# The order of one attention step in a fused attention, token-mixing and MLP kernel: products with V two pairs back, low part of x one step later, first weight blocks decoded later

## The chip, the cores and the metric

The kernel runs on one core of a Trainium2 chip. A core has a matrix engine (PE, with its weight loads shown as PEld), a vector engine (DVE), a scalar engine (ACT), GpSimd (POOL) and a queue engine (SP) that here issues the DMAs. Each engine works through its own instructions strictly in the order in which they were written, and waits at an instruction until the data that it names is there. The metric is the device time of one execution in microseconds (us); less is better. Three runs of the kernel before gave 899.58, 904.35 and 904.69 us, the median is 904.35.

## The reference

Causal attention over 4 batches and 12 heads of 64, then a mixing of tokens through rank 32, then an MLP, with two residual sums:

```python
scores = where(mask, -1e9, q @ k.T / 8)         # 4 x 12 heads, 448 x 448, causal
attn   = exp(scores - max) / (sum + 1e-9)
x      = (attn @ v), heads side by side          # 4 x 448 x 768
u      = x + (x.T @ U @ V).T                     # U 448 x 32, V 32 x 448
out    = u + relu(u @ w_ch1) @ w_ch2             # 768 -> 3072 -> 768
```

The weights arrive as 64-bit floats, so the kernel decodes each block to 32-bit words itself.

## The kernel before, in words

Heads are worked in pairs: a pair is two heads, there are 6 pairs to a batch and 24 in all. The program goes through steps n = -2, -1, 0, ...; a table called `plan` in `attention()` (L918 to L950) lists what one step does, and each entry has a lag: an entry with lag 1 works in step n on pair n - 1. The order of the entries in the table is the order of the instructions on every engine. A step before the change consists of:

- `scores` (L204), lag 0: 8 matmuls of q and k of the pair, causal blocks of 112 rows, into six PSUM banks (tiles `s`).
- `scores_max` (L228) on DVE, one for each block: it adds the mask, writes the block to SBUF (tile `p`) and takes the row maximum; `scores_exp` (L245) on ACT then takes the exponential in place and its row sum. The head of even number is called head 0, the other head 1.
- `sums_inverse` (L252) on DVE and `normalise` (L258) on POOL divide `p` by the row sums.
- `transposes` (L265), lag 1: ten PE transposes for each head into three banks (tiles `t`), which `transposed` (L275) copies to SBUF (tile `pt`), two copies of each head on ACT and one on DVE.
- `values` (L280), lag 1: the products of `pt` with V (tile `pv`); `values_out` (L310) copies them on ACT into x (tiles `xa` for batches 0 and 1, `xb` for 2 and 3).
- `x_natural` (L316), lag 2: four transposes of x (tile `xt`); `natural_high` (ACT) and `natural_low` (DVE) split it into a high part `xn_h` and a low part `xn_l`.
- `low_rank` (L331), for every second pair: 8 matmuls with U (tile `y`), with a high part on ACT and a low part on DVE. `mix` and `mix_sum` (L352 to L360): products with V of the low rank (tile `hm`), two of them in each of three steps of six, and their sum into x on DVE. `split_u` and `split_u_low` on POOL prepare x as the operand of the MLP.

The first 17 steps (n below `START`) run by themselves: this is the front of the kernel, where attention alone keeps the engines busy. What is left of the list of entries is then spread evenly over the MLP of batches 0 and 1 (`mlp()`), which yields after each half of an accumulation; that is the middle. A last part works the MLP of batches 2 and 3 in another form (`strassen()`); the change does not touch it.

Beside the plan, a list named `early` puts pieces of weight preparation into the front: `VU_AT` says at which steps the small matrices U and V are loaded, decoded and split, `W_AT` at which steps blocks 0 and 1 of the weights are decoded (`decode_bits`, L144: two passes on ACT, three on DVE; `decode_sum` on POOL) and split (`split`, one cast on ACT and one subtraction on DVE). These pieces are written directly behind the first entry of their step, so they stand ahead of that step's `scores_max` on DVE and ahead of its exponentials on ACT. In the middle each weight block is decoded in the same way, while the block before is used.

PSUM has eight banks (`bank()`); a new tile takes a bank whose tile before has been read for the last time.

Of the kernel before, what the change touches and what calls it, by code (L numbers as in the profile page):

```python
# [47 lines left out]

MIX, MIXN = 3, 2
START = 17
VU_AT = (0, 2, 2, 3)
UFREE = 60
UGAP = 3
LOADS = (13, 11, 7)
# [3 lines left out]
HE = {"d": "V", "o": "V", "13": "V", "24": "V"}  # L60
UE = {"d": "P", "o": "P", "13": "P", "24": "V"}
WL_AT = (1, 2)
W_AT = (4, 4, 5, 5, 6)


@with_exitstack
def attention_mix_mlp(ctx: ExitStack, tc: tile.TileContext, qk, v, w1, w2, vu, out):
# [48 lines left out]
    def f(ap):  # L116
        return ap.bitcast(F32)
# [6 lines left out]
    def constants():  # L124
        make_identity(nc, ident)
        nc.gpsimd.memset(mask, 0.0)
        nc.gpsimd.affine_select(
            out=mask[:, S - CP :],
            in_=mask[:, S - CP :],
            pattern=[[-1, CP]],  # L130
            compare_op=ALU.is_ge,
            fill=-8.0e9,
            base=0,
            channel_multiplier=1,
        )
# [68 lines left out]
    def scores(b, c):  # L204


        t = st.pop(("qk", b, c))
        room = {}
        for half, i in SCORES:
            h = 2 * c + half  # L210
            n = (i + 1) * CP
            key = half, BANK_OF[half][i]
            if key not in room:
                room[key] = [bank("s")[:CP], 0]
            o, at = room[key]
            room[key][1] = at + n
            o = st["o", b, h, i] = o[:, at : at + n]
            r = slice(half * D, (half + 1) * D)
            nc.tensor.matmul(  # L219
                o,  # L220
                t[r, 0, i * CP : (i + 1) * CP],
                t[r, 1, :n],
                start=True,
                stop=True,
                skip_group_check=True,
            )

    def scores_max(b, h, i):  # L228
        if ("p", b, h) not in st:
            st["p", b, h] = p_p.tile([CP, 1120], F32, tag="p", name="p")  # L230
            st["m", b, h] = p_sm.tile([CP, NT], F32, tag="m", name="m")
            st["l", b, h] = p_sm.tile([CP, NT], F32, tag="l", name="l")
        n = (i + 1) * CP
        nc.vector.tensor_tensor_reduce(  # L234
            out=st["p", b, h][:, POFF[i] : POFF[i] + n],
            in0=st.pop(("o", b, h, i)),
            in1=mask[:, S - n :],
            scale=-(D**-0.5),
            scalar=3.0e38,
            op0=ALU.add,  # L240
            op1=ALU.min,
            accum_out=st["m", b, h][:, i : i + 1],
        )
# [624 lines left out]
    def attention():  # L868


        def of_pair(f, lag):
            def steps(n):
                if 0 <= n - lag < len(pairs):
                    yield f, pairs[n - lag]

            return steps

        def of_tiles(f, half, lag, tiles):
            def steps(n):
                if 0 <= n - lag < len(pairs):  # L880
                    b, c = pairs[n - lag]
                    for i in tiles:
                        yield f, (b, 2 * c + half, i)

            return steps

        def of_head(f, half, lag):
            def steps(n):
                if 0 <= n - lag < len(pairs):
                    b, c = pairs[n - lag]  # L890
                    yield f, (b, 2 * c + half)

            return steps

        def of_two(f, lag):
            def steps(n):
                if 0 <= n - lag < len(pairs) and (n - lag) % 2:
                    b, c = pairs[n - lag]
                    yield f, (b, c // 2)

            return steps

        def mixes(f, part):
            def steps(n):
                for b in range(B):
                    for c in range(NC):
                        if n == b * NPAIR + NPAIR - 1 + MIX + c // MIXN and c % MIXN == part:
                            yield f, (b, c)

            return steps  # L910

        def only(f, *a):
            b, _ = a
            if b < 2:
                f(*a)

        first, second = (0, 2, 3, 1), (1, 3, 2, 0)
        plan = [  # L918
            of_pair(load_qk, -2),
            of_pair(scores, 0),  # L920
            of_tiles(scores_max, 0, 0, first),
            of_tiles(scores_exp, 0, 0, first),
            of_pair(x_natural, 2),
            of_pair(natural_high, 2),
            of_tiles(scores_max, 1, 0, second),
            of_head(sums_inverse, 0, 0),
            of_pair(natural_low, 2),
        ]
        for half in range(2):
            for i in range(3):  # L930
                plan.append(of_tiles(transposes, half, 1, (i,)))
                plan.append(of_tiles(transposed, half, 1, (i,)))
        plan += [
            of_tiles(normalise, 0, 0, first),
            of_tiles(scores_exp, 1, 0, second),
            of_two(low_rank, 2),
            of_two(low_rank_high, 2),
            of_two(low_rank_low, 2),
        ]
        for part in range(MIXN):  # L940
            plan += [mixes(mix, part), mixes(mix_sum, part)]
        plan += [
            of_pair(values, 1),
            of_head(sums_inverse, 1, 0),
            of_tiles(normalise, 1, 0, second),
            of_pair(values_out, 1),
            of_pair(load_v, 0),
        ]
        for part in range(MIXN):
            plan += [mixes(lambda *a: only(split_u, *a), part), mixes(lambda *a: only(split_u_low, *a), part)]  # L950
        def scores_and_max(b, c):
            scores(b, c)
            for half, i in SCORES:
                scores_max(b, 2 * c + half, i)

        def nothing(*_):
            pass

        among = {scores: scores_and_max, scores_max: nothing}
        todo = []  # L960
        for n in range(-2, len(pairs) + 8):
            for steps in plan:
                todo += [(n, f if n < START else among.get(f, f), a) for f, a in steps(n)]
        return todo

    with tc.manual_schedule():
        constants()
        early = [(n, low_rank_weights, (i,)) for i, n in enumerate(VU_AT)]
        early += [(n, load_w, (i,)) for i, n in enumerate(WL_AT)]
        for n, steps in zip(  # L970
            W_AT,
            (
# [7 lines left out]
            early += [(n, step, a) for step, a in steps]  # L980
        early.sort(key=lambda e: e[0])
        todo = attention()
        while todo[0][0] < START:
            n, step, a = todo.pop(0)
# [77 lines left out]
```

## Time and profile before

| what | value |
|---|---|
| median of three runs | 904.35 us |
| profiled execution, its own time | 902.12 us |
| its span, first to last instruction | 900.3 us |
| PE busy | 868.5 us (96%) |
| PEld, DVE, ACT, POOL busy | 84%, 76%, 53%, 35% |
| chain that ended last | PE 80%, DVE 12%, ACT 4% |
| front, 0 to 155.2 us: PE busy | 136.23 us |
| middle, 155.2 to 420 us: PE busy | 264.80 of 264.80 us |
| 420 to 460 us: PE busy | 36.31 of 40 us |
| rest, 460 to 900 us: PE busy | 431.15 of 440 us |

Busy time is the time in which an engine executes; for PE it includes matmuls that overlap, so a busy PE need not be at its peak. The chain is followed back from the last instruction, at each step to what released it. The table shows that PE stands still for 19 us in the front, for 3.7 us shortly after 420 us, and for 9 us in the last part.

### The profile page before, as it was taken

Reading aid. Unit: us, or ns where it says so; the run is one execution under the profiler, and the core shown is the slowest. Engines: PE = TensorE matmul, PEld = TensorE weight load, DVE = VectorE, ACT = ScalarE, POOL = GpSimd, SP = SyncE. Lnnn points to the kernel's source line nnn. Section 1 sums busy time; section 2 is a strip of 40 time slices with the busy share of each in tenths; the row PEclk is TensorE's granted clock in tenths of the full one; section 3 lists DMA queues with packets and bytes.
Section 4 is the critical chain, followed back from the end, with each engine's and each line's share of the span. In section 5 each row is a group of like instructions: output and inputs, shape, how many; then the busy total and the mean of one; then the engine's idle time right before and its main releaser. Section 6 shows DMA issues by size and latency. Waiting matters only on the chain.

```text
span 900.3 us, 13531 instructions
## 1 busy us (share of the span) xinstructions
PE 868.5 (96%) x4728; PEld 756.7 (84%) x4728; DVE 679.9 (76%) x1368; ACT 473.0 (53%) x1002; POOL 315.3 (35%) x342
## 2 busy tenths in 40 slices
PE   6789999999999999999899999999999999999998
PEld 4567777988889898888799999998999898898887
DVE  4766767675766776666478788789988989988896
ACT  5878887544536454355244545365463635445530
POOL 4545847423222222232114424323324323333230
PEclk9989999999999999999899999999999999999999
DMA  6135232244344433434334445612211321212103
GB/s 229 52 115 157 82 94 63 106 136 162 133 151 144 168 126 129 145 116 146 128 106 158 158 158 190 226 42 75 66 54 36 94 59 42 76 48 71 36 1 123
DMA packets 47061, 98.99 MB, mean 110 GB/s; under 512 B 4240, under 2 KB 25744, under 8 KB 46992
## 3 DMA queue, kind: packets, MB, share of 16 engines
q1 hardware_dynamic: 46992, 98.12, 33.3%
q8 instruction: 37, 0.61, 0.3%
q14 instruction: 32, 0.26, 0.1%
HBM read 73.73 MB, written 24.38 MB: 109 GB/s over the span
## 4 chain that ended last, share of the span: by engine, by line
PE 80%; DVE 12%; ACT 4%; issue 2%; DMA 1%; SPq 0%; POOL 0%; DVEq 0%; ACTq 0%
PE hf L424 20%; PE of L449 20%; PE sa L656 14%; PE se L656 7%; PE pv L288 6%; PE s L219 4%; PE sb L656 3%; DVE p L234 3%; PE t L272 3%; DVE h L470 2%; PE y L337 1%; DVE tmp L470 1%; DVE sw L470 1%; DVE xb L470 1%; DVE wsp L470 1%
## 5 line engine op out<-in xcount | busy, mean ns | idle before, releaser
L449 PE MATMUL of<-g,wsp 128*128 128x448 f32 x864 | 184.7, 369 | 0.0
L470 POOL TENSOR_TENSOR wsp<-wld,wsp 128x512 fp32r<-128x512 f32 (+1 forms) x60 | 105.2, 1762 | 215.4 <-ACT wsp L593 132.0
L449 PEld LDWEIGHTS of<-g,wsp 128*128 128x128 f32 x864 | 160.1, 188 | 14.3
L157 POOL TENSOR_TENSOR wa<-wld 128x768 int32<-128x768 int32 (+1 forms) x49 | 73.1, 1492 | 243.6 <-issue 89.7
L261 POOL TENSOR_SCALAR p<-p,r 112x112 f32<-112x112 f32 (+1 forms) x192 | 97.4, 526 | 108.9 <-DVE r L256 69.6
L248 ACT ACTIVATE p<-p,m 112x112 f32<-112x112 f32 (+1 forms) x192 | 99.8, 528 | 25.0 <-DVE m L234 25.0
L656 PE MATMUL sa<-h,wsp 128*128 128x448 f32 x432 | 98.6, 367 | 1.9 <-DVE xb L470 1.9
L424 PE MATMUL hf<-wsp 128*128 128x448 f32 x432 | 95.4, 370 | 0.0
L424 PE MATMUL hf<-u,wsp 128*128 128x448 f32 x432 | 95.4, 370 | 0.0
L656 PE MATMUL sa<-uch,wsp 128*128 128x448 f32 x288 | 89.5, 371 | 3.5 <-ACT r L677 3.5
L452 DVE TENSOR_TENSOR xa<-of,xa 128x448 f32<-128x448 f32 x96 | 59.1, 621 | 40.8 <-PE of L449 40.6
L656 PEld LDWEIGHTS sa<-h,wsp 128*128 128x128 f32 x432 | 80.6, 188 | 10.6 <-DVE xb L470 4.0
L424 PEld LDWEIGHTS hf<-u,wsp 128*128 128x128 f32 x432 | 80.7, 189 | 6.9 <-issue 0.3
L424 PEld LDWEIGHTS hf<-wsp 128*128 128x128 f32 x432 | 79.5, 188 | 7.3
L234 DVE CUSTOM_DVE_ANT_0 p<-s,mask 112x112 f32<-112x112 f32 (+2 forms) x192 | 73.2, 445 | 16.3 <-PE s L219 16.1
L175 ACT CAST wsp<-wa 128x768 fp32r<-128x768 f32 x48 | 40.1, 835 | 79.3 <-POOL wa L157 69.4
L176 DVE TENSOR_TENSOR wsp<-wa,wsp 128x768 fp32r<-128x768 f32 x48 | 50.7, 1057 | 24.7 <-ACT wsp L175 24.7
L432 ACT ACTIVATE g<-hf 128x448 fp32r<-128x448 f32 x48 | 26.1, 544 | 80.0 <-PE hf L424 80.0
L433 DVE SCALAR_TENSOR_TENSOR g<-hf,g 128x448 fp32r<-128x448 f32 x48 | 29.9, 623 | 50.4 <-ACT g L432 50.2
L288 PE MATMUL pv<-pt,v 112*64 112x336 f32 (+3 forms) x384 | 59.1, 434 | 8.5 <-DVE pt L166 6.3
L272 PE MATMUL t<-ident,p 112*112 112x112 f32 x480 | 58.0, 262 | 7.4 <-DVE m L234 4.1
L656 PEld LDWEIGHTS sa<-uch,wsp 128*128 128x128 f32 x288 | 54.0, 188 | 11.7 <-ACT r L677 6.7
(93 smaller groups left out, 1597.7 us busy)
## 6 DMA issues: line engine op xcount, KB each, us to landing
wld<-in_w_dram SPq DMA_DIRECT2D x48, 768.0 KB, 4.6
kept<-wa SPq DMA_DIRECT2D x48, 384.0 KB, 2.6
qk<-in_qk_dram SPq DMA_DIRECT2D x24, 448.0 KB, 3.5
wld<-kept SPq DMA_DIRECT2D x24, 384.0 KB, 3.2
wld<-kept SPq DMA_DIRECT2D x72, 128.0 KB, 2.4
v<-in_v_dram SPq DMA_DIRECT2D x24, 224.0 KB, 3.7
out_dram<-xa SPq DMA_DIRECT2D x12, 224.0 KB, 2.2
out_dram<-xb SPq DMA_DIRECT2D x12, 224.0 KB, 1.9
```

Source lines behind the costliest of these rows:

```text
L157: nc.gpsimd.tensor_tensor(a.bitcast(I32), t[:, :n, 1].bitcast(I32), t[:, :n, 0].bitcast(I32), op=ALU.add)
L176: nc.vector.tensor_tensor(lo, src, f(hi), op=ALU.subtract)
L234: nc.vector.tensor_tensor_reduce(out=st["p", b, h][:, POFF[i] : POFF[i] + n], in0=st.pop(("o", b, h, i)), in1=mask[:, S - n :], scale=-(D* ...
L248: nc.scalar.activation(pi, pi, AF.Exp, bias=m[:, i : i + 1], scale=-1.0, accum_out=l[:, i : i + 1])
L261: nc.gpsimd.tensor_scalar(pi, pi, r[:, i : i + 1], 1.0, op0=ALU.mult, op1=ALU.mult)
L272: nc.tensor.transpose(o[:, n : n + CP], src, ident[:CP, :CP])
L288: nc.tensor.matmul(o[j * D : (j + 1) * D, kt * CP : S], v[:, kt, j, :], pt[:, n0 : n0 + S - kt * CP], start=j not in begun, stop=not left[ ...
L424: nc.tensor.matmul(o, a[:, cs], m, start=(kc + n == 0), stop=(kc + n == NC + 1))
L449: nc.tensor.matmul(o, a[:, cs], m, start=(fc + n == 0), stop=(fc + n == FC + 1))
L452: nc.vector.tensor_tensor(x, o, x, op=ALU.add)
L470: (nc.vector if e == "V" else nc.gpsimd).tensor_tensor(o, a, b, op=op)
L656: nc.tensor.matmul(st[bank, q], a, b, start=(n in FIRST and ms[0] == 0 and k == 0), stop=(n in LAST and end and k == len(steps) - 1), skip ...
```

## The change

In a step, the products with V now belong to the pair two steps back (lag 2 in place of 1) and stand right behind the scores; the transposes of head 0 follow, then the transpose of x, then the transposes of head 1. The last two exponentials of head 1 move behind the copies of head 0. The low part of x is taken one step later (lag 3), and so are `low_rank` (lag 3) and `mix` (`MIX` 4). V is loaded one step later. `START` is 18: one step more runs in the front. U and V of the low rank are finished one step later, and the five pieces of weight decoding move from steps 4, 4, 5, 5 and 6 to steps 7 to 11.

```diff
--- before.py
+++ after.py
@@ -48,9 +48,9 @@
 
 
 
-MIX, MIXN = 3, 2
-START = 17
-VU_AT = (0, 2, 2, 3)
+MIX, MIXN = 4, 2
+START = 18
+VU_AT = (0, 2, 3, 4)
 UFREE = 60
 UGAP = 3
 LOADS = (13, 11, 7)
@@ -60,7 +60,7 @@
 HE = {"d": "V", "o": "V", "13": "V", "24": "V"}
 UE = {"d": "P", "o": "P", "13": "P", "24": "V"}
 WL_AT = (1, 2)
-W_AT = (4, 4, 5, 5, 6)
+W_AT = (7, 8, 9, 10, 11)
 
 
 @with_exitstack
@@ -914,40 +914,43 @@
             if b < 2:
                 f(*a)
 
+        def third(half):
+            plan = []
+            for i in range(3):
+                plan.append(of_tiles(transposes, half, 1, (i,)))
+                plan.append(of_tiles(transposed, half, 1, (i,)))
+            return plan
+
         first, second = (0, 2, 3, 1), (1, 3, 2, 0)
         plan = [
             of_pair(load_qk, -2),
             of_pair(scores, 0),
             of_tiles(scores_max, 0, 0, first),
             of_tiles(scores_exp, 0, 0, first),
+            of_pair(natural_low, 3),
+            of_tiles(scores_max, 1, 0, second),
+            of_tiles(scores_exp, 1, 0, second[:2]),
+            of_pair(values, 2),
+            of_pair(values_out, 2),
+            of_head(sums_inverse, 0, 0),
+            of_tiles(normalise, 0, 0, first),
+            *third(0),
+            of_tiles(scores_exp, 1, 0, second[2:]),
             of_pair(x_natural, 2),
+            of_head(sums_inverse, 1, 0),
+            of_tiles(normalise, 1, 0, second),
+            *third(1),
+            of_two(low_rank, 3),
+            of_two(low_rank_high, 3),
+            of_two(low_rank_low, 3),
             of_pair(natural_high, 2),
-            of_tiles(scores_max, 1, 0, second),
-            of_head(sums_inverse, 0, 0),
-            of_pair(natural_low, 2),
-        ]
-        for half in range(2):
-            for i in range(3):
-                plan.append(of_tiles(transposes, half, 1, (i,)))
-                plan.append(of_tiles(transposed, half, 1, (i,)))
-        plan += [
-            of_tiles(normalise, 0, 0, first),
-            of_tiles(scores_exp, 1, 0, second),
-            of_two(low_rank, 2),
-            of_two(low_rank_high, 2),
-            of_two(low_rank_low, 2),
         ]
         for part in range(MIXN):
             plan += [mixes(mix, part), mixes(mix_sum, part)]
-        plan += [
-            of_pair(values, 1),
-            of_head(sums_inverse, 1, 0),
-            of_tiles(normalise, 1, 0, second),
-            of_pair(values_out, 1),
-            of_pair(load_v, 0),
-        ]
+        plan.append(of_pair(load_v, 1))
         for part in range(MIXN):
             plan += [mixes(lambda *a: only(split_u, *a), part), mixes(lambda *a: only(split_u_low, *a), part)]
+
         def scores_and_max(b, c):
             scores(b, c)
             for half, i in SCORES:
```

On PE, in the front, a step without `low_rank` and `mix` stands before as follows (from its last two scores to its first products):

```order
L219 MATMUL s<-qk 112x224
L219 MATMUL s<-qk 112x112
L320 MATMUL xt<-ident,xa 112x128 x4
L272 MATMUL t<-ident,p 112x112 x20
L288 MATMUL pv<-pt,v 64x112
L288 MATMUL pv<-pt,v 64x224
L288 MATMUL pv<-pt,v 64x336
```

and now as follows, up to the end of its transposes:

```order
L219 MATMUL s<-qk 112x224
L219 MATMUL s<-qk 112x112
L288 MATMUL pv<-pt,v 64x112
L288 MATMUL pv<-pt,v 64x224
L288 MATMUL pv<-pt,v 64x336
L288 MATMUL pv<-pt,v 64x448 x2
L288 MATMUL pv<-pt,v 64x336
L288 MATMUL pv<-pt,v 64x224
L288 MATMUL pv<-pt,v 64x112
L272 MATMUL t<-ident,p 112x112 x10
L320 MATMUL xt<-ident,xa 112x128 x4
L272 MATMUL t<-ident,p 112x112 x10
```

The products moved from behind the twenty transposes to the place behind the scores, and the transposes of x now stand between the two heads.

On ACT, in the front, the same step before, from the copy of the products into x to the first exponential of head 1:

```order
L164 COPY xa<-pv 128x448
L248 ACTIVATE p,l<-p,m 112x112
L248 ACTIVATE p,l<-p,m 112x336
L248 ACTIVATE p,l<-p,m 112x448
L248 ACTIVATE p,l<-p,m 112x224
L324 CAST xn_h<-xt 112x4x128
L164 COPY pt<-t 112x448
L164 COPY pt<-t 112x336
L164 COPY pt<-t 112x448
L164 COPY pt<-t 112x336
L248 ACTIVATE p,l<-p,m 112x224
```

and now, from the second exponential of head 0 to the high part of x at the step's end:

```order
L248 ACTIVATE p,l<-p,m 112x336
L248 ACTIVATE p,l<-p,m 112x448
L248 ACTIVATE p,l<-p,m 112x224 x2
L248 ACTIVATE p,l<-p,m 112x448
L164 COPY xa<-pv 128x448
L164 COPY pt<-t 112x448
L164 COPY pt<-t 112x336
L248 ACTIVATE p,l<-p,m 112x336
L248 ACTIVATE p,l<-p,m 112x112
L164 COPY pt<-t 112x448
L164 COPY pt<-t 112x336
L324 CAST xn_h<-xt 112x4x128
```

The copy into x now stands behind six exponentials of its own step, and the copies of head 1 and the high part of x stand behind all eight.

On DVE, in the middle, at the end of attention (the last pair), before and now; `pt` is the copy of head 1's last transposes, `xn_l` the low part of x, L150 to L152 the decoding of a weight block:

```order
L433 SCALAR_TENSOR_TENSOR g<-hf,g 128x448
L150 TENSOR_SCALAR wa<-wa 128x768
L151 TENSOR_SCALAR wa<-wa 128x768
L152 SCALAR_TENSOR_TENSOR wld<-wld,wa 128x768
L166 COPY pt<-t 112x336
L329 TENSOR_TENSOR xn_l<-xt,xn_h 112x4x128
```

```order
L433 SCALAR_TENSOR_TENSOR g<-hf,g 128x448
L150 TENSOR_SCALAR wa<-wa 128x768
L151 TENSOR_SCALAR wa<-wa 128x768
L152 SCALAR_TENSOR_TENSOR wld<-wld,wa 128x768
L329 TENSOR_TENSOR xn_l<-xt,xn_h 112x4x128
L350 TENSOR_TENSOR y<-y 64x256
```

The copy that stood behind the decoding of a block is now a whole block earlier, and the low part of x stands in its place.

## Rows read from the trace of the kernel before

**Rows 1.** Busy time by stretch: stretch, us; per engine busy us (xinstructions); granted clock, DMA.

```profile
420.00:460.00 40.00, 36.31 (x188) 31.89 (x188) 19.84 (x33) 13.81 (x22) 7.75 (x8) 0.91 0.28 95
```

**Rows 2.** The chain of waits, steps 14 and 15: start us, us, what.

```profile
129.70 2.08 PE s L219 x12
131.78 0.58 PE xt L320 x4
132.36 1.92 PE t L272 x20
...
143.08 1.09 PE y L337 x7
144.17 0.21 PE hm L355
...
144.99 2.04 PE pv L288 x10
```

**Rows 3.** Timeline of step 12: start us, us, instruction, count, [idle before <- releaser].

```profile
113.41 2.15 PE L219 MATMUL s<-qk 64*112 64x112 f32 x16
...
114.57 0.28 DVE L234 CUSTOM_DVE_ANT_0 p<-s,mask 112x112 f32<-112x112 f32 x1 [0.79 <-PE s L219]
...
114.89 0.39 ACT L248 ACTIVATE p<-p,m 112x112 f32<-112x112 f32 x1 [0.83 <-DVE m L234]
...
117.01 0.56 ACT L324 CAST xn_h<-xt 112x512 fp32r<-112x512 f32 x1
...
117.48 1.64 ACT L164 COPY pt<-t 112x448 f32<-112x448 f32 x4
...
117.84 0.66 DVE L329 TENSOR_TENSOR xn_l<-xt,xn_h 112x512 fp32r<-112x512 f32 x1
...
119.02 2.47 PE L288 MATMUL pv<-pt,v 112*64 112x112 f32 x16 [0.96 <-ACT pt L164]
```

**Rows 4.** Timeline of step 15, DVE: low part of y, two sums into x.

```profile
145.69 0.43 DVE L350 TENSOR_TENSOR y<-y 64x256 fp32r<-64x256 f32 x1 [1.83 <-ACT y L346]
146.15 1.16 DVE L360 TENSOR_TENSOR xa<-hm,xa 128x448 f32<-128x448 f32 x2
```

**Rows 5.** Timeline, first maxima of steps 1 and 2, decoding of U and V.

```profile
11.71 0.24 DVE L234 CUSTOM_DVE_ANT_0 p<-s,mask 112x112 f32<-112x112 f32 x1
...
20.02 0.73 ACT L149 ACTIVATE wa<-wld 128x576 f32<-128x576 f32 x1
...
22.46 0.27 DVE L234 CUSTOM_DVE_ANT_0 p<-s,mask 112x112 f32<-112x112 f32 x1
```

**Rows 6.** Timeline of steps 4 and 5: decoding and splitting of weight block 0.

```profile
39.33 0.92 ACT L149 ACTIVATE wa<-wld 128x768 f32<-128x768 f32 x1
...
43.01 0.28 DVE L234 CUSTOM_DVE_ANT_0 p<-s,mask 112x112 f32<-112x112 f32 x1
...
47.40 4.41 PE L288 MATMUL pv<-pt,v 112*64 112x112 f32 x16 [1.22 <-DVE pt L166]
...
52.27 0.83 ACT L175 CAST wsp<-wa 128x768 fp32r<-128x768 f32 x1
...
53.14 0.96 DVE L176 TENSOR_TENSOR wsp<-wa,wsp 128x768 fp32r<-128x768 f32 x1 [3.13 <-ACT wsp L175]
```

**Rows 7.** Timeline of the middle, start, in PE's row.

```profile
155.19 2.09 PE L424 MATMUL hf<-wsp 128*128 128x448 f32 x9
```

**Rows 8.** Timeline of the middle, around the last pair's products.

```profile
435.53 0.41 PE L288 MATMUL pv<-pt,v 112*64 112x112 f32 x2
...
439.06 0.50 DVE L166 COPY pt<-t 112x336 f32<-112x336 f32 x1
...
439.62 3.99 PE L288 MATMUL pv<-pt,v 112*64 112x224 f32 x14 [3.69 <-DVE pt L166]
...
443.54 2.75 PE L424 MATMUL hf<-u,wsp 128*128 128x448 f32 x9
...
446.49 2.07 PE L424 MATMUL hf<-u,wsp 128*128 128x448 f32 x9
```

## The prediction, made before the changed kernel was run

> **What bounds the kernel now.** I read the stretches first, then the waits of PE, then the timeline where PE waits. By the table above PE is busy 96% of the span, and in the middle, from 155 to 420 us, without a gap, so there the order of attention cannot matter: what is moved into the middle or out of it counts with its PE time alone. Idle PE time that this change can touch lies in two places. One is the front, up to the first MLP matmul at 155.19 us [rows 7]. The other is one stall after 435 us: the products of the last pair wait 3.69 us for a copy of DVE that stands behind the decoding of a weight block, and the 14 products and nine MLP matmuls behind it take 3.99 and 2.75 us [rows 8]; the granted clock of that stretch is 0.91 [rows 1], so PE ran part of it at the lower of its two levels. The last part is not touched.
>
> **PE work of a step.** Scores 2.08, transposes of x 0.58, transposes of p 1.92, products 2.04 [rows 2]: 6.62 us. Every second step adds 1.09 for the low rank, three steps of six add four matmuls of 0.2 for the mix [rows 2]. A plain step takes 8.1 us before (113.41 to the end of its products at 119.02 + 2.47, [rows 3]), because the products wait 0.96 us for copies on ACT. The change takes that wait away: products of two pairs back have had their operands for a step.
>
> **The new step, scheduled by hand.** Let 0 be the start of its first maximum on DVE. Scores start 1.16 earlier and the first exponential 0.32 later [rows 3]. Four exponentials take 2.12, the high part of x 0.47, four copies 1.50 (starts of the ACT rows in [rows 3]; the copies end at 118.98, just ahead of the products). Eight maxima and two small DVE operations take 3.27 (114.57 to 117.84), some 1.45 for each head.
> - DVE: maxima of head 0 to 1.45; low part of x (0.66 long, 0.6 until the next) to 2.05; maxima of head 1 to 3.5.
> - ACT: exponentials of head 0 from 0.32 to 2.44; two of head 1 can follow their maxima until about 3.65; copy into x to 4.1 (the products ended at 2.08 + 2.04 - 1.16 = 2.96); two copies of head 0 to 4.85; last two exponentials to 5.8; two copies of head 1 to 6.55; high part of x to 7.0.
> - PE: transposes of x from 4.2 to 4.75, of head 1 to 5.7; then the next scores, so the next zero is at 5.7 + 1.16 = 6.85.
> - DVE again: reciprocal of head 1 behind the last exponential, copy of head 1, free at 6.65; then 0.43 for the low part of y, 1.16 for two sums [rows 4].
>
> So the next zero comes at 6.85 in a plain step, 7.95 with low rank (PE), 7.85 with mix (DVE), 8.85 with both (DVE). I add 0.3 to each for the handovers between engines that the sum of starts leaves out: 7.15, 8.25, 8.15, 9.15. ACT is the tightest: it ends its step at 7.0, the next exponential is due 0.32 after the next zero.
>
> **The front.** Step 1 has its first maximum at 11.71 [rows 5], which the change leaves alone. Behind it ACT needs 0.32, eight exponentials (4.24) and four copies (1.50): 17.75; then U and V are decoded, which takes 2.44 from ACT to the first maximum of step 2 (20.02 to 22.46, [rows 5]): 20.2 instead of 22.46, since no copy into x stands ahead. Fifteen spacings follow to step 17: the first without a low part 6.95, four plain 28.6, five with low rank 41.25, three with mix 24.45, two with both 18.3, together 119.55. Weight preparation comes on top, as it stands ahead of the maxima. A block's decoding takes 3.68 from ACT's first pass to the first maximum [rows 6]; it starts when ACT is free, so step 7 comes at 7.7 + 3.68 and not at 8.25, which costs 3.1, and step 10 at 7.0 + 3.68 and not at 8.15: 2.5. A split takes 0.83 on ACT and 0.96 on DVE [rows 6]: step 9 pays 1.3; the three splits of U and V in step 4, of about the same number of columns, I put at 2.2. Together 9.1. Sums on POOL hide behind its idle time; the loads of V find a buffer that was freed a step earlier and have a whole step to land, so they cost nothing, and if that cover went the products alone would wait. Step 17 begins at 20.2 + 119.55 + 9.1 = 148.85, and PE is through with it 6.8 later, at 155.65. That is 0.45 later than before, but one step's scores, transposes and transposes of x (2.08 + 1.92 + 0.58 = 4.58) have been taken out of the middle. **Gain of the front: 4.1 us.** Its bounds: handovers of 0 give 4.5 us more, of 0.6 each 4.5 less.
>
> **The stall after 435 us.** The last pair's products now come a step behind its copies, so their wait goes. What is late next: the low part of the last x. It now stands behind the decoding that held up the copy, and nine MLP matmuls after its transposes PE wants it. Decoding ended 439.06 - 435.53 = 3.53 us after the MLP accumulation ahead of it [rows 8]; then 0.66 for the low part [rows 3]: 4.2. PE gets there after 0.58 + 2.0 and a first matmul of 0.2, so it waits about 1.5 instead of 3.69, a gain of 2.2. The 14 products should take 14/16 of 2.04, that is 1.8, not 3.99, and the nine matmuls 2.07 as at 446.49 [rows 8], not 2.75: 2.9 more if the clock stays up behind the shorter wait. I take 4.9 (2.2 + 2.9, less 0.2 for a second short wait for the high part); the bounds are 0 (the same stall in another place) and 6.6 (no stall).
>
> **Sum.** 4.1 + 4.9 = 9.0 us. The profiled execution took 902.12 us, so 893.1; the median of the runs is 2.2 above it, which gives **895 us**. About 1% is what a measurement of this kernel can tell from no change, and 1% of the median is 9.0: the forecast stands on that line.
>
> **Rivals.**
> - *PE alone bounds the front* (13%): the ACT chain is shorter than I have it, and the step falls to its PE work of 6.62, 7.71, 7.42 and 8.51. That is 0.3 to 0.75 less in each of 15 steps, some 8.7 us, and a third of the preparation hides as well: 12 us, **883 us**. For it speaks that PE's work, not ACT's, is the longest sum in a step with low rank; against it that the copy into x stands behind six exponentials.
> - *The clock falls in the front* (12%). Step 4 before shows it: behind a wait of 1.22 us the products take 4.41 us [rows 6] and not 2.04. In the new front DVE and ACT are held by preparation in steps 2, 4, 7, 9 and 10, and PE waits 1 to 3 us in each. If the clock falls in every one, each costs 2.4 for the products or what stands there, and some tenths for the scores, about 2.65: 13 us, **908 us**, slower than before. It decides from a wait of the size of that in step 4 on. Against it: step 4 decoded a block and summed it in the same step, which now takes two, and the new waits are partly spread over the step. "TensorE: Matmul & The Clock Gate" in the Trainium skill, section "HAM oscillation — how this bites in real kernels", says that a matrix engine that waits some microseconds between short rounds of work starts each round at half the clock; by that rule this rival would be the likely one and the time its 908. The trace agrees for step 4 and speaks against it for step 12, where the products behind a wait of 0.96 us took 2.47 and not 4.41 [rows 3, 6].
> - *Too few PSUM banks* (15%). The tile of x's transposes is now held into the next step, until DVE takes the low part, so seven of eight banks serve scores, products and transposes, and the fourth to sixth bank of the scores wait for the copies of head 1, the last on ACT. I have them free at 6.55, when the scores want them at 6.5 to 7. If ACT is later by 0.6 in each step, 16 steps lose 9.6: **905 us**, again above the profiled execution. "Perfetto Trace Analysis" in the Trainium skill, section "Identifying Performance Opportunities", says that an equal gap that repeats can mean too little PSUM for the next tile; it would show as that. By it the sum would be this rival's.
> - *The stall stays* (10%): the wait for the low part brings the clock down as the old one did, and only the front gains: **900 us**.
>
> The forecast itself has 50%, with 890 to 900 for its own range. The range for 8 in 10 leaves out the lower half of the first rival and the upper parts of the second and third: **886 to 906 us**. Faster by over 1% (below 895.3): half of the forecast and nearly all of the first rival, 0.37. Slower by over 1% (above 913): the far end of the clock rival, 0.05. Within 1%: 0.58.
>
> **What would show it.** In the profile after: the first MLP matmul near 155.6 us; no wait of the products for copies; steps of 7.2 to 9.2 us; a short wait of the transposes of x for ACT in each; steps 7, 9 and 10 longer by 1 to 3 us; about 1.5 us of waiting of the low rank after 430 us with the clock at 1.0. A plain step above 7.8 us, or a front that ends after 160 us, would prove the schedule wrong; a granted clock under 0.95 in the front, the second rival; a new wait in the middle, where I count none, would upset the rest.

## The result, and the profile after

The changed kernel takes **907.52 us** (median of 20 runs, 902.97 to 910.79); 20 runs of the kernel before beside it gave 902.15 us (897.12 to 904.69). The ratio is **1.0061**, with a 95% interval of 1.0046 to 1.0076: slower by 0.6%, where 895 us and a gain were forecast. The profiled execution took 908.52 us, 15.4 more than the 893.1 of the forecast's sum.

The first rows to read are those that answer to [rows 7] and [rows 1]. In the timeline of PE, the first MLP matmul:

```profile
165.26 1.98 PE L424 MATMUL hf<-wsp 128*128 128x448 f32 x9
```

The front ends 10.07 us later than at 155.19 us [rows 7], though only 4.58 us of work came into it. From there to the end of the span it is now 741.4 us (906.7 - 165.3), and it was 745.1; with those 4.58 us taken out it should have been 740.5 with the old stall still in it. So the front lost 5.5 us where 4.1 were to be gained, and the part behind it lost 0.9 where 4.9 were to be gained.

Busy time of PE by stretch, in the kernel after; the column behind the count is the granted clock:

```profile
20.00:40.00 20.00, 16.96 (x116) 0.83 0.24 75
40.00:60.00 20.00, 17.67 (x137) 0.91 0.26 87
60.00:80.00 20.00, 16.80 (x125) 0.91 0.26 74
80.00:100.00 20.00, 15.71 (x126) 0.98 0.40 125
100.00:120.00 20.00, 16.83 (x111) 0.84 0.42 125
120.00:140.00 20.00, 19.63 (x155) 0.93 0.27 85
140.00:160.00 20.00, 19.64 (x158) 1.00 0.24 71
...
440.00:460.00 20.00, 14.90 (x66) 0.83 0.29 99
```

The clock is below 1.0 in every stretch from 20 to 140 us. The waits of PE in the front, each row with its total in us, how often it occurs, and the longest (of the first row, 2.30, 2.15, 2.16, 1.72 and 2.17 us stand in steps 2, 4, 7, 9 and 10):

```profile
PE xt L320 <- ACT xa L164: 11.6, 11, 2.3
...
PE pv L288 <- DMA v<-in_v_dram: 3.0, 1, 3.0
```

Step 10 shows the first of them, in the timeline of PE:

```profile
96.16 1.26 PE L272 MATMUL t<-ident,p 112*112 112x112 f32 x10 [0.40 <-DVE m L234]
99.59 1.10 PE L320 MATMUL xt<-ident,xa 128*112 128x128 f32 x4 [2.17 <-ACT xa L164]
100.48 2.07 PE L272 MATMUL t<-ident,p 112*112 112x112 f32 x10
102.23 0.56 PE L337 MATMUL y<-xn_h,um_s 112*128 112x256 f32 x1
```

The transposes of x wait 2.17 us for the copy on ACT, as step 10 has its exponentials behind the decoding of a block. What follows runs at the lower of the two clock levels: four transposes of x in 1.10 us (0.65 in a step that is not disturbed), ten transposes of p in 2.07 (1.12).

Step 12 shows the second, in the timeline of POOL, SP and PE:

```profile
109.41 1.46 POOL L157 TENSOR_TENSOR wa<-wld 128x768 int32<-128x768 int32 x1
...
110.90 0.33 SPq L395 DMA_DIRECT2D kept<-wa  x1
...
111.33 0.37 SPq L141 DMA_DIRECT2D wld<-in_w_dram  x1
...
111.79 0.42 SPq L201 DMA_DIRECT2D v<-in_v_dram  x1
...
113.63 2.15 PE L219 MATMUL s<-qk 64*112 64x112 f32 x16
...
118.76 3.25 PE L288 MATMUL pv<-pt,v 112*64 112x112 f32 x16 [2.98 <-DMA v<-in_v_dram]
```

SP issues in the order of the program. The store of a decoded block (`kept`) waits for the sum on POOL, and the next weight load and V's load stand behind it. V is issued at 111.79 and its products, now right behind the scores, can start at 118.76 only: 2.98 us of waiting, then 3.25 us for what takes 2.11. The record of that one load (L201) says when it landed:

```profile
DMA to landing us min/median/max: 6.8/6.8/6.8
```

It landed at 118.62, and the products start 0.14 us later.

The same happens where the old stall was, which answers to [rows 8]; SP and PE, kernel after:

```profile
437.16 0.33 SPq L395 DMA_DIRECT2D kept<-wa  x1
...
437.64 0.33 SPq L141 DMA_DIRECT2D wld<-in_w_dram  x1
438.02 0.46 SPq L201 DMA_DIRECT2D v<-in_v_dram  x1
...
443.54 3.76 PE L288 MATMUL pv<-pt,v 112*64 112x112 f32 x16 [4.08 <-DMA v<-in_v_dram]
...
452.01 0.39 PE L337 MATMUL y<-xn_h,um_s 112*128 112x256 f32 x1 [0.43 <-ACT xn_h L324]
...
453.52 0.38 PE L337 MATMUL y<-xn_l,um_s 112*128 112x256 f32 x1 [1.12 <-DVE xn_l L329]
...
454.74 3.26 PE L424 MATMUL hf<-u,wsp 128*128 128x448 f32 x9
```

The wait of 3.69 us for a copy [rows 8] has become one of 4.08 us for V. The low rank then waits 0.43 us for the high part and 1.12 for the low part, 1.55 together, where the forecast had about 1.5 for the low part and 0.2 for the high.

### The profile page after: what moved, and what is told of

Read it like the earlier page. It is cut to its first block, busy times and chain, and to the rows that moved or that the text cites. A ratio compares the mean times of both kernels' runs of the same rounds, so it can differ in the third digit from the quotient of the medians.

```text
span 906.7 us, 13562 instructions
## 1 busy us (share of the span) xinstructions
PE 868.4 (96%) x4728; PEld 759.0 (84%) x4728; DVE 681.3 (75%) x1368; ACT 474.9 (52%) x1002; POOL 318.8 (35%) x342
## 4 chain that ended last, share of the span: by engine, by line
PE 39%; DVE 9%; ACT 2%; issue 1%; DMA 1%; SPq 0%; DVEq 0%; ACTq 0%
PE sa L656 13%; PE of L449 7%; PE hf L424 7%; PE se L656 7%; PE sb L656 3%; DVE h L470 2%; DVE tmp L470 1%; DVE sw L470 1%; DVE xb L470 1%; DVE wsp L470 1%; ACT h L478 1%; DVE r L470 1%; DMA v<-in_v_dram 1%; ACT wsp L593 0%; PE pv L288 0%
## 5 line engine op out<-in xcount | busy, mean ns | idle before, releaser
L261 POOL TENSOR_SCALAR p<-p,r 112x112 f32<-112x112 f32 (+1 forms) x192 | 99.7, 538 | 106.6 <-DVE r L256 55.2
L272 PE MATMUL t<-ident,p 112*112 112x112 f32 x480 | 63.2, 272 | 3.7 <-POOL p L261 2.1
L656 PEld LDWEIGHTS sa<-uch,wsp 128*128 128x128 f32 x288 | 54.0, 188 | 11.6 <-ACT r L677 6.6
L593 ACT CAST wsp<-sw 128x256 fp32r<-128x256 f32 (+3 forms) x60 | 33.9, 576 | 55.2 <-DVE sw L470 25.8
```

The lines of the kernel that those rows point to most:

```text
L261: nc.gpsimd.tensor_scalar(pi, pi, r[:, i : i + 1], 1.0, op0=ALU.mult, op1=ALU.mult)
L272: nc.tensor.transpose(o[:, n : n + CP], src, ident[:CP, :CP])
L656: nc.tensor.matmul(st[bank, q], a, b, start=(n in FIRST and ms[0] == 0 and k == 0), stop=(n in LAST and end and k == len(steps) - 1), skip ...
```

## The experiments

One theory was to be told apart from its rivals. **A:** the front and the part around 440 us each lose by V's load, which stands behind the store, and the front besides by the lower clock behind the waits of the transposes of x; the two losses are separate. Rivals: the waits themselves are the loss and the clock costs nothing; the place of the weight preparation is the loss. Ratios are to the kernel before, run on the same chip; the changed kernel stands at 1.0061.

**V's load at the front of the step** (`v_first`).

```diff
         plan = [
+            of_pair(load_v, 1),
             of_pair(load_qk, -2),
...
-        plan.append(of_pair(load_v, 1))
```

> The changed kernel with the load of V written at the very front of a step, ahead of that step's store of a decoded block, and nothing else different. Theory A (V's load is held on SP's queue behind the store of the decoded block, and that is what the products wait 3.0 us for in step 12 and 4.1 us at 443.5): both waits go, the products behind them return to about 2.0 and 1.8 us, step 12 to 13 falls from 12.2 to 8.2 to 9 us, and the time is 7 to 11 us under the changed kernel, 897 to 901 us, level with the kernel before or a little under it. The waits of the transposes of x (2.3, 2.15, 2.16, 1.72 and 2.17 us) stay as they are. Rival B (the load is late for another reason, a buffer or the DMA itself, or the steps are bound by something just behind it): the wait moves to another instruction of the same step, the first MLP matmul stays within 1 us of 165.3, and the time stays within 3 us of 907.5.

Measured: 897.40 us, ratio 0.9954 (0.9936 to 0.9971). Both waits for V are gone; V of step 12 is now issued at 95.89 us, so its buffer was free by then, 15.9 us before the changed kernel issued it. The front ends at 160.00 us, step 12 lasts 7.95 us in place of 12.20, and from the front's end to the end of the span it is 734.8 us in place of 741.4. PE around the last pair, with V's load in time:

```profile
433.89 2.11 PE L288 MATMUL pv<-pt,v 112*64 112x112 f32 x16
...
442.24 0.39 PE L337 MATMUL y<-xn_l,um_s 112*128 112x256 f32 x1 [1.14 <-DVE xn_l L329]
...
443.17 1.99 PE L424 MATMUL hf<-u,wsp 128*128 128x448 f32 x9
```

The products take 2.11 us and the nine MLP matmuls behind the low rank's wait 1.99, at the upper level. So V's load cost 5.3 us in the front and 6.6 behind it, 11.9 between the two profiled spans; rival B falls. The 6.6 holds for this pair of profiles: in the three other pairs below that differ in V's load alone (with dummies, with the transposes of x last, with early preparation) the part behind the front differs by 2.8, 7.5 and 12.9 us.

**Dummy matmuls in the waits** (`warm`).

```diff
+WARM = (2, 4, 7, 9, 10)
...
         o = st["xn", b, c] = bank("xt")[:CP].rearrange("p (s n) -> p s n", s=NT)
+        if b * NPAIR + c + 2 in WARM:
+            for _ in range(3):
+                nc.tensor.matmul(
+                    o.rearrange("p s n -> p (s n)")[:, :S], ident[:CP, :CP], mask,
+                    start=True, stop=True, skip_group_check=True,
+                )
         for s in range(NT):
```

> The changed kernel with three dummy fp32 matmuls of 448 columns (identity times the mask, results overwritten) ahead of the transposes of x in steps 2, 4, 7, 9 and 10, where those wait 1.7 to 2.3 us for the copy on ACT; the waits themselves stay. Theory A (the front's excess of some 7 us in these steps is the lower clock behind the waits): the granted clock stays near 1.0 from 20 to 120 us, the ten transposes behind them return to 0.9 to 1.0 us from 2.1 and the scores to 2.1 from 3.0 to 3.6, the first MLP matmul comes 4 to 7 us earlier than 165.3, and the time is 900 to 904 us. Rival C (the waits are the loss, and PE would wait for ACT or DVE next even at the higher clock): the clock rises but the first MLP matmul stays within 1.5 us of 165.3 or comes later by what the dummies take, and the time is 906 to 912 us.

Measured: 903.07 us, ratio 1.0008 (0.9994 to 1.0022); the front ends at 160.27, 5.0 us earlier. The granted clock is 1.00 from 20 to 100 us, and 0.83 from 100 to 120, where the products now wait 3.55 us for V instead of 2.98. Theory A stands, rival C falls.

**Both edits** (`v_first_warm`).

> Both edits of the two kernels ahead in one: V's load at the front of the step, and three dummy matmuls ahead of the transposes of x in steps 2, 4, 7, 9 and 10. If the two losses are separate, as theory A has it, the gains add: 11 to 17 us under the changed kernel, 890 to 896 us, near the 893 to 895 that the hand schedule gave. If one hides the other (the rivals B and C), the time is no lower than the better one of the two alone.

Measured: 890.55 us, ratio **0.9881** (0.9866 to 0.9896): the gains add, and a little more, 17.0 us where the two alone give 10.1 and 4.5. The front ends at 152.76 us. Stretches of PE, as above, with both edits:

```profile
20.00:40.00 20.00, 19.19 (x138) 1.00 0.27 89
40.00:60.00 20.00, 19.64 (x157) 1.00 0.26 86
60.00:80.00 20.00, 19.06 (x144) 1.00 0.38 122
80.00:100.00 20.00, 19.84 (x138) 1.00 0.18 54
100.00:120.00 20.00, 19.41 (x160) 1.00 0.56 174
```

The first MLP matmul, with V's load first and with both edits:

```profile
160.00 1.98 PE L424 MATMUL hf<-wsp 128*128 128x448 f32 x9
```

```profile
152.76 1.99 PE L431 MATMUL hf<-wsp 128*128 128x448 f32 x9
```

Since this kernel differs from the one with V's load first by the dummies alone, the lower clock of the front is worth 160.00 - 152.76 = 7.2 us. With V late it is worth only 5.0 (165.26 - 160.27), and V's load costs 7.5 beside the dummies (160.27 - 152.76) where it cost 5.3 without: when the steps get shorter, V is waited for longer. The two losses are separate in cause, but not independent in size. The spacings of the first maxima show where the clock's share lies (us; each is from the start of a step's first maximum on DVE to that of the next step's; only steps whose next step has no preparation on ACT or DVE, and the forecast is that of the step by itself):

| step | forecast | after | V first | V first, dummies | V first, x late |
|---|---|---|---|---|---|
| 2 | 6.95 | 8.98 | 8.98 | 6.80 | 6.48 |
| 4 | 8.25 | 9.48 | 9.48 | 8.17 | 7.45 |
| 7 | 7.15 | 8.52 | 8.41 | 7.22 | 6.66 |
| 10 | 9.15 | 11.64 | 10.28 | 9.06 | 8.53 |
| 12 | 8.25 | 12.20 | 7.95 | 7.97 | 7.47 |
| 13, plain | 7.15 | 7.00 | 7.00 | 7.01 | 6.66 |
| 14, low rank | 8.25 | 7.97 | 7.98 | 7.96 | 7.46 |
| 15, mix | 8.15 | 7.83 | 7.83 | 7.83 | 7.73 |
| 16, both | 9.15 | 8.85 | 8.86 | 8.86 | 8.53 |

**Early weight preparation in the new order** (`decode_early`).

```diff
-VU_AT = (0, 2, 3, 4)
+VU_AT = (0, 2, 2, 3)
...
-W_AT = (7, 8, 9, 10, 11)
+W_AT = (4, 4, 5, 5, 6)
```

> The new order of a step with the pieces of weight preparation where the kernel before had them (U and V of the low rank in steps 0, 2, 2, 3, blocks 0 and 1 in steps 4, 4, 5, 5, 6). Theory A: what costs is each step in which preparation makes PE wait at the transposes of x, wherever it stands; now steps 2 to 6 pay and steps 7 to 11 run at 7.0 to 8.9 us with the clock at 1.0, and no store stands ahead of V's load late in the front. Step 4, with both pieces of a block, waits 3 us or more. The first MLP matmul comes at 160 to 164 us, the stall near the end of the attention stays, and the time is 902 to 907 us. Rival D (the later decoding is the whole loss of the front): the first MLP matmul at 156 to 158 us and the time 898 to 900 us. Rival E (the late place of the decoding was a gain, as in the forecast): the time is over 910 us.

Measured: 903.54 us, ratio 1.0028 (1.0016 to 1.0041). The front ends at 154.70 us, below what rival D gave it, and yet the time is that of theory A: neither had both. In the front no products wait for V, and the disturbed steps are next to each other, steps 2 to 6. Behind it, the wait for V takes 4.3 us, and 2.43 us come at the last part's first matmuls, for a sum of DVE that stands behind weight preparation there; none of the kernels in which V is loaded first waits more than 0.63 us there. The matmuls from 460 to 580 us were slower by 2% besides (below, under the hardware).

**Early preparation with V's load first** (`v_first_early`), and with dummies in steps 2 to 5 (`v_first_early_warm`, with `WARM = (2, 3, 4, 5)`).

> V's load at the front of the step, and the weight preparation in the steps of the kernel before (0, 2, 2, 3 and 4, 4, 5, 5, 6): the two single edits that each gained, together. Theory A (the losses are separate): the front ends at 154 to 156 us as with the early preparation alone, the stall of 4.3 us after 425 us goes with the slow products behind it, and the time is 5.3 us under the kernel with V's load first alone (its front ended at 160.0): 891 to 894 us. Rival F (what the early preparation gains in the front is given back later, as with it alone, where the front was 10.6 us shorter and the time only 4.0): 895 to 899 us, the difference between the end of the front and the last part, 2 to 5 us, being visible behind 460 us.

> The kernel ahead with three dummy matmuls ahead of the transposes of x in steps 2, 3, 4 and 5, where they waited 1.1 to 2.2 us with the early preparation alone. Theory A: the granted clock is near 1.0 from 20 to 80 us (0.87 to 0.96 without dummies), the front ends at 148 to 151 us, and the time is 4 to 6 us under the kernel ahead: 886 to 890 us by theory A for both, 890 to 894 with rival F. Rival C (the waits are the loss, not the clock): no gain over the kernel ahead.

Measured: 893.12 us, ratio 0.9904 (0.9884 to 0.9924), front end 156.18; and 891.53 us, 0.9885 (0.9867 to 0.9903), front end 152.68. The first lies within theory A's range. The second gains 3.5 us in the front, where an end at 148 to 151, that is 5 to 8 us, was expected, and 1.6 us of time where 4 to 6 were; the two intervals overlap. The clock is at 1.00 from 20 to 160 us. With dummies the front ends at 152.7 us with the preparation early or late (152.68 and 152.76), so what sets the two places apart is the clock alone: 7.2 us in the late place, 3.5 in the early one. Dummies bring the clock back, not the waits.

**Late decoding in the old order** (`decode_late_only`): the kernel before with `W_AT = (7, 8, 9, 10, 11)`.

> The kernel before, with its own order of a step, where only the weight decoding is moved to steps 7 to 11. Theory A (each step in which preparation makes PE wait costs some 2 us and its clock, wherever it stands, and spread out there are more such steps than crowded): the front ends 0 to 4 us later than 155.2, steps 4 and 5 run at 8.0 to 9.3 us, steps 7, 9 and 10 at 9.5 to 13, and the time is 902 to 907 us. Rival E (late decoding is a gain, as the forecast took it): the front ends before 153 us and the time is under 900 us. Rival H (late decoding costs only in the new order, through V's load): the time stays within 1 us of 902.

Measured: 900.03 us, ratio 0.9985 (0.9969 to 1.0000). The front ends at 156.29, 1.1 us later, as theory A had it, but the time is 1.8 us lower and not up to 5 higher, which also misses rival H's 901 to 903; no theory had both. In the old order too V's load, again behind a block's store and a weight load (issued at 111.77 us, landed 6.9 later), now makes the products wait, 1.87 us at 118.85. What is sure is that the later decoding by itself is worth a few tenths of a per cent at most.

**The transposes of x behind those of head 1, with V's load first** (`x_late`).

```diff
-            of_pair(x_natural, 2),
             of_head(sums_inverse, 1, 0),
             of_tiles(normalise, 1, 0, second),
             *third(1),
+            of_pair(x_natural, 2),
```

> V's load at the front of the step, and the transposes of x moved behind those of head 1, with no dummies. If the wait for the copy on ACT is what lowers the clock (theory A), useful work of 0.96 us now stands in that wait, it falls from some 2.2 us to 1.2 us or less, the clock falls in fewer of the steps 2, 4, 7, 9 and 10, and the front ends 2 to 6 us earlier than 160.0: 892 to 896 us. Rival G (the transposes of head 1 cannot start either, since their banks wait for copies that stand behind the same work on ACT): the wait moves to them with the same length, the clock falls as before, and the time stays within 2 us of 897.4 or is longer, by 0.3 to 0.5 us in each plain step, as the high part of x is then the last thing in a step.

Measured: **886.07 us**, ratio 0.9825 (0.9808 to 0.9841), more than any theory gave; the front ends at 147.21. Step 10, PE:

```profile
88.23 1.26 PE L272 MATMUL t<-ident,p 112*112 112x112 f32 x10 [1.01 <-DVE m L234]
89.69 1.26 PE L272 MATMUL t<-ident,p 112*112 112x112 f32 x10 [0.19 <-DVE xn_l L329]
91.66 0.65 PE L320 MATMUL xt<-ident,xa 128*112 128x128 f32 x4 [0.71 <-ACT xa L164]
92.07 0.36 PE L337 MATMUL y<-xn_h,um_s 112*128 112x256 f32 x1
```

PE still stands for 1.91 us in this step, but in three pieces with twenty transposes between them, and the transposes of x take 0.65 us and not 1.10. The granted clock is 1.00 from 40 to 160 us (0.97 from 20 to 40). The plain step falls to 6.66 us, which is PE's own work in [rows 2], 6.62: the first rival's state, "PE alone bounds the front", reached by another edit. That rival put the front 12 us under the forecast's 155.65; here it is 8.4 under it. Of the 5.5 us by which the front is shorter than with dummies, some 3.4 lie in steps that had no dummies (by the spacings, such as 6.66 for 7.01 in step 13): the gain over the dummies lies for the larger part outside the steps with the long waits.

**The same edit without V's load first** (`x_late_only`).

> The changed kernel with one edit: the transposes of x stand behind those of head 1. V's load stays behind the store of the decoded block. Theory A (the wait for the copy on ACT with its clock, and V's late load, are two separate losses): the gain of the other order is that which it gave beside the moved load, 11 us (897.4 to 886.1), so 894 to 899 us; the waits of the products for V's load stay, some 3 to 5 us in step 12 and 3 to 5 us near the end of the attention, since the steps ahead are shorter and the store is no earlier. Rival J (V's load was late only because the steps were long, or the order alone makes both losses go): under 890 us, no wait for V.

Measured: 902.23 us, ratio 1.0008 (0.9995 to 1.0021): above theory A's range, and rival J falls outright. The front came forward by 11.6 us, to 153.67, as expected, but the time by only 5.3 (the profiled execution, 899.24 us, is the fastest of twelve, so the trace shows less than the median lost). The waits for V in the front take more now that the steps are shorter: 3.23 us in step 12, and another in step 9 that bears a wrong name. SP and PE, and the record of that load of V:

```profile
70.96 0.33 SPq L395 DMA_DIRECT2D kept<-wa  x1
...
71.86 0.43 SPq L201 DMA_DIRECT2D v<-in_v_dram  x1
...
78.70 3.54 PE L288 MATMUL pv<-pt,v 112*64 112x112 f32 x16 [2.67 <-DVE m L234]
```

```profile
DMA to landing us min/median/max: 6.7/6.7/6.7
```

The row names a maximum on DVE, which ended just ahead of the products. But in the kernel with V first, which differs by V's load alone, the same products start 2.1 us behind their scores, while those maxima still run. V was issued at 71.86 here and landed 6.7 us later, at 78.56; the products start 0.14 us behind that, the same distance as in the waits that name V. So this wait is for V again. Behind the front there are 3.60 us of waiting for V, and 2.42 us ahead of the last part, as with the early preparation alone.

**The same edits with early preparation** (`x_late_early`).

> V's load at the front of the step, the transposes of x behind those of head 1, and the weight preparation in the steps of the kernel before (0, 2, 2, 3 and 4, 4, 5, 5, 6). With the clock no longer falling, the late and the early place should cost nearly the same: the front ends at 145 to 149 us (147.2 with the late place) and the time is 884 to 889 us. If early preparation gains by itself, as the step from 897.4 to 893.1 us without the x edit would say, the front ends before 145 us and the time is 881 to 884 us.

Measured: **884.15 us**, ratio **0.9807** (0.9792 to 0.9821), front end 146.77: 1.9% faster than the kernel before and the best of all. It lies within the first case of the expectation, though the clock still fell here, to 0.91 from 40 to 60 us; its interval overlaps that of the same kernel with late preparation (`x_late`), so the place of the preparation is no longer told apart.

**Weight loads away from V's load** (`w_later`): in the changed kernel, blocks 2 and 3 are loaded in steps 9 and 12 in place of 8 and 11.

```diff
-                [(decode_w, (0, 1)), (load_w, (2,))],
-                [(decode_w, (0, 2))],
+                [(decode_w, (0, 1))],
+                [(decode_w, (0, 2)), (load_w, (2,))],
...
-                [(decode_w, (1, 1)), (load_w, (3,))],
+                [(decode_w, (1, 1))],
...
+        early.append((12, load_w, (3,)))
```

> The changed kernel with the loads of weight blocks 2 and 3 moved from steps 8 and 11 to steps 9 and 12 in the front, so that V's load of steps 8 and 11 still stands behind the store of a decoded block but no longer behind a weight load of 768 KB. It splits the wait of 2.98 us in step 12: V was issued at 111.79 us and its products started at 118.76. Theory K (the transfer is slow since it runs beside the weight load): V is issued about 0.45 us earlier and lands in 3 to 4 us, the wait in step 12 is under 0.5 us, the front ends 3 to 4 us earlier than 165.3, and the time is 903 to 905 us, as the wait near the end of the attention stays. Theory L (the issue behind the store alone makes it late): the wait falls only by the 0.45 us, to 2.3 to 2.8, and the time stays within 1.5 us of 907.5.

Measured: 903.40 us, ratio 1.0010 (0.9995 to 1.0024), front end 159.68. SP and PE in steps 11 and 12:

```profile
109.79 0.33 SPq L395 DMA_DIRECT2D kept<-wa  x1
110.21 0.38 SPq L201 DMA_DIRECT2D v<-in_v_dram  x1
...
114.41 2.11 PE L288 MATMUL pv<-pt,v 112*64 112x112 f32 x16
```

The record of this load of V:

```profile
DMA to landing us min/median/max: 3.1/3.1/3.1
```

Theory K: V is still issued behind the store, 0.42 us after it, lands in 3.1 us, and nothing waits; the weight load is issued 1.0 us behind it. With the weight load 0.46 us ahead it took 6.8 us. So step 12 was late for two reasons that had to meet: the store put V's load late, and the weight load just ahead of it made its transfer slow. The part behind the front does not change (741.6 us): the wait there stays, 4.40 us. Of the 5.6 us in the front, 4.2 are step 12; most of the other 1.4 lies in steps 2 and 3, where the program is the same as in the changed kernel; no experiment here explains that part.

## Why the prediction failed, point by point

- **The step that failed first** is "the loads of V find a buffer that was freed a step earlier and have a whole step to land, so they cost nothing". The buffer was free, but the load was not issued when it became free: its place in SP's order is behind `kept`, and the products had moved from a step's end to just behind its scores. Price: 5.3 us in the front, 6.6 us behind it. The forecast did say that without this cover the products alone would wait, and they do; the term was put at nothing by the free buffer and the step's length, and SP's order was not part of the reasoning. With V's load first it was issued 15.9 us earlier.
- **The second** is the chance of the rival that the clock falls in the front. It had 12% and it happened, in four of the five steps named (step 9 waited 1.72 us and paid nothing). Its price was 7.2 us, not 13: 2.2, 1.3, 1.2 and 1.2 us in steps 2, 4, 7 and 10 and the rest in the steps behind them, where 2.65 each stood. The forecast worked out these waits, 1 to 3 us, and then left out what comes behind them. "TensorE: Matmul & The Clock Gate" in the Trainium skill, section "HAM oscillation — how this bites in real kernels", tells of a matrix engine that waits some microseconds for DMA between short rounds of work and starts each round at half the clock. The traces agree in kind, for shorter waits for another engine and for a part of a step only: behind 2.17 us the level was lower, and filling the waits with work took that away. The rival's price and its condition came from one row, the products behind a wait of 1.22 us in step 4. That row does not stand alone; a longer wait is just ahead of it in the kernel before:

```profile
43.78 2.40 PE L272 MATMUL t<-ident,p 112*112 112x112 f32 x16 [1.88 <-DVE m L234]
```

So that 1.22 us by itself lowers the clock is not shown; in the new order 1.72 us did not. That the total came out close to that rival's 908 is chance: more than half of the loss (11.9 of 19.1 us) is V's load.
- **The hand schedule** was right, to 4% in a step. Undisturbed steps take 7.00, 7.97, 7.83 and 8.85 us where 7.15, 8.25, 8.15 and 9.15 stood; 0.15 for handovers and not 0.3 fits the plain one. (Of its readings one is off by 0.1: the four copies end at 119.12 by [rows 3], 118.98 is where the next exponential starts; and 17.75 should be 17.77. Nothing rests on either.) With V in time and the clock up, the front ends at 152.76, 2.9 us before the 155.65 of the forecast.
- **The stall near 440 us.** The products' wait for copies went and the low rank waits 1.55 us, both as forecast; the new wait, for V, was not seen. With V's load first the part behind the front is 734.8 us; against 745.1 less 4.58 that is a gain of 5.7 where 4.9 were forecast. The agreement is in part luck: some 580 MLP matmuls from 460 to 580 us took 207 ns each in the profile before and 203 in this one and in that of the changed kernel (below, under the hardware), an estimated 2.3 us that no run ties to the order. Without it the gain is 3.4, and the loss behind the front in the changed kernel 3.2 and not 0.9.
- **The sum.** The front: 7.2 for the clock and 5.3 for V, less 2.9 for the schedule, is the 9.6 us between +4.1 and -5.5. Behind it: 6.6 for V, less 0.8, is the 5.8 between +4.9 and -0.9. Together 15.4, which is all of the miss between the profiled executions; the pieces are differences of single profiles, so that they add up is no proof of each. The 2.2 us that the forecast added from the profiled execution to the median were chance: over 20 runs the median of the kernel before is 902.15, and its profiled execution took 902.12.
- **The other rivals.** Too few PSUM banks: no wait of the scores for a bank, and the undisturbed steps are shorter than forecast. PE alone as the bound: not in the changed kernel (7.00 against 6.62), but in those with the transposes of x at the end. The stall stays: it did, at 4.08 us, but for V and not for the low part. The middle has no wait of PE from 180 to 420 us, as forecast.

## What to carry to other kernels

A load costs nothing only when its place in the issuing queue is free too: look at what stands ahead of it there, what that waits for, and which large transfer runs beside it, before a consumer is moved forward. A wait of PE costs its length and can cost the clock of what stands behind it (four of the five waits of 1.7 to 2.3 us in the changed kernel did). Cut it into pieces by moving work of PE's own into it: the clock came back as with dummies, it needs no extra work, and here it also made the undisturbed steps shorter (886.07 against 890.55 us). When a change loses, repair one loss at a time before it is given up: this order is 0.6% slower as written and 1.75% faster with two of its entries moved.

## What the hardware showed that was not expected

- The same wait does not always lower the clock. In six kernels without a wait for V, the low rank between 428 and 443 us waits the same 1.1 us for the same instruction; the nine MLP matmuls behind it take 1.99 to 2.00 us in four of them and 3.14 and 3.44 in the two others. Kernels with equal instructions can differ there by over a microsecond.
- The MLP matmuls between 460 and 580 us run at one of two rates within a whole profiled execution: 203 ns each (for instance after, `v_first`, `warm` and `x_late`) or 207 ns (before, `v_first_warm`, `decode_early`, `x_late_early`), both at a granted clock of 1.00. Over such a stretch that is about 2 us; what sets it stays open.
- The two kernels with the transposes of x at the end and V's load first scatter less: 885.29 to 886.37 and 883.99 to 884.92 us in four runs each, where the two others with four runs spread over 2.6 and 3.2 us. That the missing waits are the reason is not shown; waits of up to 2.23 us are left in the faster of the two.
